# First layer in tiles of 512 columns, with all its work in one written order, on one Trainium2 core

## The chip, the core and the metric

The kernel is one program on one core of a Trainium2 chip. Five engines run their own instruction queues: PE (matrix multiply), DVE and ACT (vector and scalar work), POOL (a further elementwise engine), SP (which only issues DMAs here). An engine never leaves the order of its queue; an instruction that waits for a semaphore holds all behind it. The metric is the time of the program on the device in microseconds.

## What is computed

Attention of two kinds is added, then two feed-forward layers follow on 2304 tokens of 512 channels, all in float32:

```
# B, H, S, D = 4, 8, 576, 64; pooled: means over 4 tokens (144 per batch)
out_d = softmax(q_d k_d^T / 8) v_d            # pooled, per batch and head
local = softmax(q k^T / 8, |i - j| < 4) v      # 7 keys for each token
x     = repeat(out_d, 4) + local               # 2304 tokens x 512
h = x @ w_in; g = relu(h)**2; x2 = g @ w_out   # first layer, 2048 wide
y = ((x2 @ w_a) * (x2 @ w_b)) @ w_o2           # second layer, 1536 wide
```

The weights and the operands of the big products are split into a high and a low part, and a product is three matmuls: high by high, high by low, low by high (`PASSES`).

## The kernel before

**Tiles.** The first layer runs in nine tiles of 256 token columns. In each tile there are 16 steps f. Step f is `Hidden` (12 matmuls, line 598, into a PSUM bank), its `high` on ACT (relu, square and rounding, lines 606, 607, 609), its `low` on DVE (line 612), and, two steps later, `project` (12 matmuls, line 619, into two banks that collect over the 16 steps, two column blocks of 256 in each). The operands of a tile are the tiles `xx`; the result x2 goes to DRAM by way of `x2sb` (`x_d<-x2sb`), but for the last tile's, which stays on the chip (`xr`).

**Attention.** The first two tiles' local attention runs on PE (`Block`: scores, softmax, transposes, values); that of the other seven (`Local`) runs on DVE (products and sums, lines 379, 388, 419) and POOL (additions, lines 427 to 429) with its transposes on PE (line 436). Pooled attention (`Pooled`) runs once for each of four batches, in four pairs of heads: scores on PE (241, 256), minimum on DVE (268), exponentials with an accumulator read on ACT (278), division on ACT, POOL or DVE (293, 296), transposes (305) and values (319) on PE, copies on ACT or DVE. Its sums over 4 tokens are made by DMAs that add to what lies in the tile; POOL issues these (line 224). For batch 0 q and k go in two halves: `qkd` and two tiles `more`, each loaded by SP and added to by POOL's DMA, then joined by an addition (line 230).

**Weights.** Those of the first layer come packed; `wd` loads one of 32 pieces, `wc`, `wa`, `wh` and `wl` turn it into high and low parts on ACT, DVE and POOL.

**What sets the order.** A list of tokens (`ORDER`, 464 of them) gives the program order of the start and the first two tiles: block attention (`bq` to `bl`), batch 0 and part of batch 1 of the pooled attention (`pl` to `po`), the weights, and the steps `H`, `J` (`high`), `L` (`low`), `P` (`project`). From the third tile on a loop runs `H`, `J`, `L`, `P` for each step, and events by step number (`at_iteration`) place one piece of pooled or local attention beside each. Beside the last tile the second layer is prepared: its first weights are decoded (`wb`) and the first 1024 columns of x2 are loaded back (`x2s<-x_d`) and split (`xb`). The second layer runs in 512 columns (line 911), with sums and differences of blocks so that seven block products take the place of eight; ACT copies its banks out (line 1007, `r`), and among its first copies stand the splits of the next 1024 columns.

**PSUM.** Eight banks of 2 KB a partition: three for `Hidden`, two for the projection, three for attention. The first layer's banks are closed before the second layer opens its own eight.

## Time and profile before

| | us |
|---|---|
| median of 3 runs | 944.28 (943.98 to 947.16) |
| the profiled execution | 943.94 |
| its span, first to last instruction | 942.2 |
| first matmul of the first layer that is followed by more | 71.35 |
| first matmul of the second layer | 540.20 |

| busy in the span | us | share |
|---|---|---|
| PE | 891.4 | 95% |
| DVE | 620.4 | 66% |
| ACT | 480.7 | 51% |
| POOL | 355.3 | 38% |

The mean granted clock of PE over the span is 0.979 of full speed. A share over the whole span mixes three stretches: the attention of the start, the first layer, and the second layer; they are read apart below. Time that an engine other than PE is idle counts only where PE waits for it.

### The profile page before, as it was taken

The page shows a single profiled execution, that of the slowest core. Times are in us where ns is not written, and L with a number is a line of the kernel's source. Part 1 is how long each engine was busy: PE and PEld are TensorE (multiplying, and loading weights), DVE is VectorE, ACT ScalarE, POOL GpSimd, SP SyncE. Part 2 cuts the span into 40 slices and gives each one's busy share as a digit, 9 for nine tenths or more (in the row PEclk, how much of TensorE's full clock was granted, in tenths as well). Part 3 has the DMA queues.
Part 4 walks back from the last instruction along what each step waited for, and adds up shares of the span by engine and source line. Part 5 has one row for each costly group of instructions (what it writes and reads, how often), then busy time and mean ns, then how long its engine had stood idle before and what let it go on. Part 6 is the DMA issues. An engine that isn't in the chain of part 4 may idle for free.

```text
span 942.2 us, 16371 instructions
## 1 busy us (share of the span) xinstructions
PE 891.4 (95%) x6130; PEld 811.0 (86%) x6130; DVE 620.4 (66%) x892; ACT 480.7 (51%) x1232; POOL 355.3 (38%) x321
## 2 busy tenths in 40 slices
...
GB/s 312 168 164 248 263 115 90 155 140 65 81 63 204 99 82 63 74 71 69 96 90 103 120 50 190 267 275 201 226 211 184 254 168 351 387 407 357 227 101 79
DMA packets 69888, 161.86 MB, mean 172 GB/s; under 512 B 8472, under 2 KB 16920, under 8 KB 69808
## 3 DMA queue, kind: packets, MB, share of 16 engines
...
q8 instruction: 48, 0.79, 0.4%
q14 instruction: 32, 0.26, 0.1%
...
## 4 chain that ended last, share of the span: by engine, by line
PE 78%; DVE 6%; DMA 6%; ACT 4%; POOL 3%; issue 2%; ACTq 0%; SPq 0%; DVEq 0%; POOLq 0%
PE bank L911 39%; PE bank L619 18%; PE bank L598 18%; DMA more<-in_qk_p 2%; DMA raw<-in_w_in 1%; PE bank L241 1%; DMA wo<-wo_d 1%; DVE pv L419 1%; DMA ys<-y_d 1%; DVE p L379 1%; DVE g L612 1%; ACT a L278 1%; DMA qkd<-in_qk_p 1%; DVE raw L156 1%; POOL pv L428 1%
## 5 line engine op out<-in xcount | busy, mean ns | idle before, releaser
L598 PE MATMUL bank<-xx,w 128*128 128x256 f32 x1728 | 236.5, 287 | 10.2 <-DVE g L612 3.5
L619 PE MATMUL bank<-g,w 128*128 128x256 f32 x1728 | 233.8, 285 | 0.8 <-POOL w L167 0.4
L598 PEld LDWEIGHTS bank<-xx,w 128*128 128x128 f32 x1728 | 220.8, 194 | 14.1 <-DVE g L612 4.7
L911 PE MATMUL bank<-xb,wb 128*128 128x512 f32 x1008 | 230.4, 389 | 0.7 <-DVE r L961 0.5
L911 PEld LDWEIGHTS bank<-xb,wb 128*128 128x128 f32 x1008 | 188.6, 188 | 40.3 <-DVE r L961 1.5
L619 PEld LDWEIGHTS bank<-g,w 128*128 128x128 f32 x1728 | 216.3, 191 | 5.0 <-issue 2.9
L911 PE MATMUL bank<-op,wo 128*128 128x512 f32 (+1 forms) x648 | 132.1, 366 | 1.6 <-DVE op L772 1.6
L911 PEld LDWEIGHTS bank<-op,wo 128*128 128x128 f32 x648 | 111.9, 189 | 21.9 <-DVE op L772 2.3
L612 DVE TENSOR_TENSOR g<-bank,g 128x256 fp32r<-128x256 f32 x144 | 60.1, 420 | 99.5 <-ACT g L609 98.8
L427 POOL TENSOR_TENSOR pv<-pv 128x768 f32<-128x768 f32 x28 | 55.1, 1967 | 179.6 <-DVE pv L419 179.6
L606 ACT ACTIVATE bank<-bank 128x256 f32<-128x256 f32 x144 | 53.3, 370 | 120.3 <-PE bank L598 120.2
L772 POOL TENSOR_TENSOR wb<-raw,wb 128x256 fp32r<-128x256 f32 x96 | 83.0, 883 | 64.0 <-ACT wb L851 60.5
L1007 ACT ACTIVATE r<-bank 128x512 f32<-128x512 f32 x72 | 43.0, 597 | 93.8 <-PE bank L911 84.8
L772 DVE TENSOR_TENSOR op<-ys,op 128x512 fp32r<-128x512 f32 x84 | 54.0, 707 | 31.3 <-ACT op L775 31.3
L156 DVE SCALAR_TENSOR_TENSOR raw<-raw,signs 128x512 uint32<-128x512 uint32 x68 | 57.6, 852 | 25.1 <-ACT signs L129 23.4
L961 DVE TENSOR_TENSOR r<-bank,r 128x512 f32<-128x512 f32 x48 | 32.8, 686 | 43.9 <-PE bank L911 31.0
L419 DVE TENSOR_TENSOR pv<-vt,sc 128x1792 f32<-128x1792 f32 x28 | 58.6, 2100 | 3.0 <-POOL x L429 3.0
L775 ACT ACTIVATE op<-ys 128x512 fp32r<-128x512 f32 x84 | 47.1, 624 | 25.6 <-PE bank L911 15.0
L379 DVE TENSOR_TENSOR p<-qt,kt 128x1792 f32<-128x1792 f32 x28 | 60.2, 2149 | 0.0
L609 ACT ACTIVATE g<-bank 128x256 fp32r<-128x256 f32 x144 | 55.4, 385 | 4.6
L388 DVE TENSOR_REDUCE sc<-p 128x28 f32<-128x1792 f32 x28 | 56.1, 2004 | 0.0
L772 POOL TENSOR_TENSOR wos<-raw,wos 128x256 fp32r<-128x256 f32 x48 | 43.6, 924 | 31.5 <-ACT wos L851 29.4
...
## 6 DMA issues: line engine op xcount, KB each, us to landing
...
y_d<-r SPq DMA_DIRECT2D x72, 256.0 KB, 2.0
wo_d<-wos SPq DMA_DIRECT2D x48, 256.0 KB, 2.4
...
wo<-wo_d SPq DMA_DIRECT2D x24, 256.0 KB, 7.5
...
```

The source lines that it names most:

```text
L156: nc.vector.scalar_tensor_tensor(out=self.v, in0=self.v, scalar=13, in1=self.signs, op0=ALU.logical_shift_right, op1=ALU.bitwise_or,)
L379: nc.vector.tensor_tensor(out=self.p, in0=q.unsqueeze(2).to_broadcast([P, FACTOR, WIN, D]), in1=window(k), op=ALU.mult,)
L388: nc.vector.tensor_reduce(out=self.s[:, :, h], in_=self.p, axis=AX.X, op=ALU.add)
L419: nc.vector.tensor_tensor(out=p, in0=window(heads.pop(("v", n))), in1=self.s[:, :, h].unsqueeze(3).to_broadcast([P, FACTOR, WIN, D]), op=A ...
L427: add(out=p[:, :, 0:3], in0=p[:, :, 0:3], in1=p[:, :, 4:7], op=ALU.add)
L598: nc.tensor.matmul(out=h, lhsT=wi[f].w[:, a, ct * P:(ct + 1) * P], rhs=x_rhs(i, ct, b), start=(n == 0), stop=(n == 3 * NCT - 1),)
L606: nc.scalar.activation(out=h, in_=h, func=AF.Relu)
L609: nc.scalar.activation(out=self.g[:, 0], in_=h, func=AF.Copy)
L612: nc.vector.tensor_tensor(out=self.g[:, 1], in0=self.h, in1=self.g[:, 0].bitcast(F32), op=ALU.subtract)
L619: nc.tensor.matmul(out=x2[et // 2][:, et % 2 * T1:(et % 2 + 1) * T1], lhsT=wo[f].w[:, a, et * P:(et + 1) * P], rhs=g[:, b], start=(f == 0 ...
L772: engine.tensor_tensor(out=out, in0=in0, in1=in1, op=ALU.subtract)
L911: nc.tensor.matmul(out=out, lhsT=blk[:, a, cols:cols + P], rhs=rhs[b], start=(start and n == 0), stop=(stop and n == 2), skip_group_check= ...
```

## The change

**Tiles.** The first layer now runs in five tiles: 512, 256, 512, 512 and 512 columns (`TILES`). Two or one of the 256-token pieces of attention make the operands of one tile. Each of the 16 steps is again 12 + 12 matmuls. `Hidden` alternates between two PSUM banks, the projection collects in four (one for each 128 channels), attention has two. `project` does the passes with the high part of g first, then those with the low part; the first `Hidden` of a tile does the same with its operands.

**Blocks.** Three pieces of local attention run on PE (`BLOCKS`); `Local` runs for pieces 3 to 8.

**Order.** One list of 1197 tokens sets the order of everything up to the second layer: also all pooled and local attention, the evictions of x2 (`E`), its stores (`D`), the opening of the second layer's pools (`Q`), the parts of its preparation (`F`), and the last 256 columns' halves (`rh`, `rl`). The loop and its events are gone. In the last tile, pieces 7 and 8 end together: piece 7 is stored, piece 8 stays on the chip.

**Loads.** All loads of the start are issued by SP (before, ACT issued some of them). Pooled q and k of batch 0 are eight plain loads and six additions; the other batches keep the adding DMAs.

The core of the diff:

```diff
-PE_TILES = 2
+BLOCKS = 3
+TILES = ((0, 2), (2, 1), (3, 2), (5, 2), (7, 2))
+LAST = len(TILES) - 1
...
-        def add_more(self, n, j):
-            src = qk_p[self.b, j][:, n * NCT * SG:(n + 1) * NCT * SG]
-            self.add_to(self.more[n], src, j % 2)
...
+        def get(self, n, j, queue):
+            if j == 0:
+                out = (self.qd, self.kd)[n]
+            else:
+                out = self.more[n, j] = wp.tile([P, NCT * SG], F32, tag="w", name="more")
+            queue.dma_start(out=out, in_=qk_p[self.b, j][:, n * NCT * SG:(n + 1) * NCT * SG])
 
-        def join(self, n, engine):
+        def join(self, n, j, engine):
             d = (self.qd, self.kd)[n]
-            engine.tensor_tensor(out=d, in0=d, in1=self.more[n], op=ALU.add)
+            engine.tensor_tensor(out=d, in0=d, in1=self.more.pop((n, j)), op=ALU.add)
...
     class Hidden:
-        def __init__(self, i, f):
-            self.h = h = bank("h")[:, :T1]
...
+        def __init__(self, t, f):
+            width = TILES[t][1] * T1
+            self.h = h = bank((t * F1 + f) % 2)[:, :width]
+            todo = [(ct, a, b) for ct in CTS[t] for a, b in PASSES]
+            if f == 0:
+                todo.sort(key=lambda z: z[2])
+            for n, (ct, a, b) in enumerate(todo):
+                nc.tensor.matmul(
+                    out=h, lhsT=wi[f].w[:, a, ct * P:(ct + 1) * P], rhs=xT[t, ct][:, b],
...
+    def project(t, f):
         if f == 0:
-            x2[i] = [bank(kind) for kind in kinds]
...
+            width = TILES[t][1] * T1
+            x2[t] = [bank(2 + et)[:, :width] for et in range(NCT)]
+        g = hid.pop((t, f)).g
+        todo = [(et, a, 0) for et in range(NCT) for a in range(2)] + [(et, 0, 1) for et in range(NCT)]
+        for et, a, b in todo:
...
+    def store(t, e2):
+        i, count = TILES[t]
+        if t == LAST:
+            count -= 1
+            src, ets = x2sb[t, 0], slice(0, NCT)
```

**Three places in the order.** First, POOL at the start. `qkd` and `more` are pooled q and k, `vd` pooled v, `blk` the blocks' exponentials; a DMA row is an issue, and the DMAs on POOL add to what lies there. Before:

```order
L224 DMA more<-in_qk_p 128x576
L224 DMA vd<-in_v_p 72x1024
L224 DMA qkd<-in_qk_p 128x1152
L224 DMA more<-in_qk_p 128x576
L527 TENSOR_TENSOR blk<-blk,den 128x560
L230 TENSOR_TENSOR qkd<-qkd,more 128x576
L527 TENSOR_TENSOR blk<-blk,den 128x560
```

Now:

```order
L1377 DMA vd<-in_v_p 72x1024
L1390 TENSOR_TENSOR qkd<-qkd,more 128x576
L1685 TENSOR_TENSOR blk<-blk,den 128x560
L1390 TENSOR_TENSOR qkd<-qkd,more 128x576 x3
L1685 TENSOR_TENSOR blk<-blk,den 128x560 x2
L1350 TENSOR_TENSOR w<-raw,w 128x512
L1377 DMA vd<-in_v_p 72x1024
```

The adding DMAs for q and k are gone from here, and three more joins have come; the loads they join are SP's rows:

```order
L1379 DMA vd<-in_v_p 72x1024
L1386 DMA qkd<-in_qk_p 128x576 x2
L1386 DMA more<-in_qk_p 128x576 x3
L1624 DMA qb<-in_q_t 128x1024
L1628 DMA kb<-in_k_t 128x524 x2
L1630 DMA band<-in_mask 128x140
L1386 DMA more<-in_qk_p 128x576 x3
L1330 DMA raw<-in_w_in 128x2047
```

`raw` is a piece of weights; before, SP's first rows held one part of each (`more`, `vd`, `qkd`, `raw`, `more`), and the rest came by POOL.

Second, PE in the middle of the first layer. L1766 and L1801 are `Hidden` and `project` of the new code (before L598 and L619), L1399 pooled scores, L1453 and L1591 transposes of pooled and local attention (before L305 and L436), L1467 pooled values. Before, from the third tile on, in this manner:

```order
L598 MATMUL bank<-xx,w 128x256 x12
L305 MATMUL bank<-ident,a 72x72 x4
L619 MATMUL bank<-g,w 128x256 x12
L598 MATMUL bank<-xx,w 128x256 x12
L305 MATMUL bank<-ident,a 72x72 x4
L436 MATMUL xps<-ident,x 128x128 x4
L619 MATMUL bank<-g,w 128x256 x12
L598 MATMUL bank<-xx,w 128x256 x12
L619 MATMUL bank<-g,w 128x256 x12
L598 MATMUL bank<-xx,w 128x256 x12
L319 MATMUL bank<-aT,vd 64x144 x4
L256 MATMUL bank<-qkd 72x144 x4
```

Now, between the last projection of the second tile and the first hidden matmuls of the third:

```order
L1591 MATMUL bank<-ident,x 128x128 x4
L1399 MATMUL bank<-qkd 72x144 x4
L1453 MATMUL bank<-ident,a 72x72 x8
L1467 MATMUL bank<-aT,vd 64x144 x4
L1453 MATMUL bank<-ident,a 72x72 x8
L1467 MATMUL bank<-aT,vd 64x144 x4
L1591 MATMUL bank<-ident,x 128x128 x4
L1467 MATMUL bank<-aT,vd 64x144 x4
L1453 MATMUL bank<-ident,a 72x72 x8
L1467 MATMUL bank<-aT,vd 64x144 x4
L1591 MATMUL bank<-ident,x 128x128 x4
L1766 MATMUL bank<-xx,w 128x512 x24
```

The attention pieces, which stood one or two at a time between groups of twelve, stand in a row here; ahead of this piece are the tile's last 36 projections with eight pooled score matmuls and eight transposes between them. The ends of the first and the third tile have like rows; at the end of the fourth only three groups of four transposes stand between the last projections.

Third, the border of the layers. On SP, `x_d<-x2sb` stores x2, `x2s<-x_d` loads it back, `raw` are weights. Before:

```order
L644 DMA x_d<-x2sb 128x2x256 x2
L349 DMA vt<-in_v_l 128x640 x2
L147 DMA raw<-in_w_a 128x2047 x2
L789 DMA x2s<-x_d 128x512 x8
L644 DMA x_d<-x2sb 128x2x256 x2
L147 DMA raw<-in_w_b 128x2047 x2
L789 DMA x2s<-x_d 128x512 x8
L147 DMA raw<-in_w_a 128x2047 x2
L147 DMA raw<-in_w_b 128x2047 x2
L955 DMA y_d<-r 128x512 x5
```

Now:

```order
L1330 DMA raw<-in_w_b 128x2047 x2
L1830 DMA x_d<-x2sb 128x2x512
L1877 DMA x2s<-x_d 128x512 x8
L1830 DMA x_d<-x2sb 128x2x512
L1330 DMA raw<-in_w_a 128x2047 x2
L1830 DMA x_d<-x2sb 512x1x256
L1877 DMA x2s<-x_d 128x512 x8
L1330 DMA raw<-in_w_a 128x2047 x2
L1330 DMA raw<-in_w_b 128x2047 x2
L2081 DMA y_d<-r 128x512 x5
```

The last store (512x1x256: piece 7, all channels) stands ahead of the second eight loads, and weights and a store that stood elsewhere lie around it. On ACT, `r` is the copy of a second-layer bank, `xb` the split of x2. Before:

```order
L609 ACTIVATE g<-bank 128x256
L851 ACTIVATE wb<-raw 128x256
L775 ACTIVATE xr_6532<-bank 128x512
L775 ACTIVATE xr_6535<-bank 128x512
L1007 ACTIVATE r<-bank 128x512
L775 ACTIVATE xb<-x2s 128x512 x2
L1007 ACTIVATE r<-bank 128x512
L775 ACTIVATE xb<-x2s 128x512 x2
L1007 ACTIVATE r<-bank 128x512
L775 ACTIVATE xb<-x2s 128x512 x2
```

Now:

```order
L1296 ACTIVATE x2sb<-bank 128x256
L1939 ACTIVATE wb<-raw 128x256
L1838 ACTIVATE xr_4762<-bank 128x256 x2
L1296 ACTIVATE x2sb<-bank 128x256 x2
L1838 ACTIVATE xr_4770<-bank 128x256 x2
L2133 ACTIVATE r<-bank 128x512
L1863 ACTIVATE xb<-x2s 128x512 x2
L2133 ACTIVATE r<-bank 128x512
L1863 ACTIVATE xb<-x2s 128x512 x2
L2133 ACTIVATE r<-bank 128x512
```

Evictions of the last tile (`x2sb`) have come in ahead of the second layer's first copy; the copies and splits behind are in the order of before.

## Rows read from the trace of the kernel before

**Rows 1.** The page's chain of work that ended last, by line

```profile
PE bank L911 39%; PE bank L619 18%; PE bank L598 18%; DMA more<-in_qk_p 2%; DMA raw<-in_w_in 1%; PE bank L241 1%; DMA wo<-wo_d 1%; DVE pv L419 1%; DMA ys<-y_d 1%; DVE p L379 1%; DVE g L612 1%; ACT a L278 1%; DMA qkd<-in_qk_p 1%; DVE raw L156 1%; POOL pv L428 1%
```

**Rows 2.** Busy time by stage: stretch, its length, busy us (instructions), granted clock, DMA

```profile
71.35:150.00 78.65, 70.58 (x528) 65.25 (x528) 60.22 (x87) 55.24 (x146) 32.37 (x28) 0.92 0.69 204
150.00:540.20 390.20, 386.77 (x3273) 380.16 (x3273) 270.04 (x355) 198.99 (x568) 156.86 (x116) 1.00 0.35 96
```

**Rows 3.** Timeline of PE at full clock: start, duration, line, tiles, count

```profile
499.88 1.60 PE L598 MATMUL bank<-xx,w 128*128 128x256 f32 x12
501.32 1.60 PE L619 MATMUL bank<-g,w 128*128 128x256 f32 x12
...
613.79 15.57 PE L911 MATMUL bank<-xb,wb 128*128 128x512 f32 x68
629.21 5.92 PE L911 MATMUL bank<-xr,wb 128*128 128x256 f32 x48
```

**Rows 4.** The page's costliest groups, first layer: busy, mean, idle before

```profile
L598 PE MATMUL bank<-xx,w 128*128 128x256 f32 x1728 | 236.5, 287 | 10.2 <-DVE g L612 3.5
L619 PE MATMUL bank<-g,w 128*128 128x256 f32 x1728 | 233.8, 285 | 0.8 <-POOL w L167 0.4
```

**Rows 5.** The chain that ended last, in order of time, at the start

```profile
18.80 13.47 DMA more<-in_qk_p
...
67.29 5.97 DMA qkd<-in_qk_p
```

**Rows 6.** Timeline of POOL at the start

```profile
32.40 1.40 POOL L230 TENSOR_TENSOR qkd<-qkd,more 128x576 f32<-128x576 f32 x1 [9.43 <-DMA more<-in_qk_p]
33.76 1.31 POOL L527 TENSOR_TENSOR blk<-blk,den 128x560 f32<-128x560 f32 x1
```

**Rows 7.** Timeline of PE: pooled scores, and the first layer's first matmuls

```profile
37.82 1.98 PE L241 MATMUL bank<-qkd 64*72 64x144 f32 x12
...
71.35 1.44 PE L598 MATMUL bank<-xx,w 128*128 128x256 f32 x5 [1.95 <-DVE xx L580]
...
77.09 5.28 PE L598 MATMUL bank<-xx,w 128*128 128x256 f32 x29 [0.37 <-POOL xx L580]
```

**Rows 8.** The page's DMA rate in 40 slices of the span

```profile
GB/s 312 168 164 248 263 115 90 155 140 65 81 63 204 99 82 63 74 71 69 96 90 103 120 50 190 267 275 201 226 211 184 254 168 351 387 407 357 227 101 79
```

**Rows 9.** Timeline of ACT: four normalising operations of one pooled head pair

```profile
131.39 1.32 ACT L293 ACTIVATE a<-a,den 72x144 f32<-72x144 f32 x4
```

**Rows 10.** Groups by form: line, engine, tiles, count, busy us, mean ns, idle

```profile
L278 ACT ACTIVATE a<-bank,mx 72x144 f32<-72x144 f32 x64 | 23.5, 372 | 22.4 <-DVE mx L268 22.3
...
L268 DVE TENSOR_REDUCE mx<-bank 72x2 f32<-72x288 f32 x32 | 14.2, 445 | 10.6 <-PE bank L241 10.5
...
L278 ACT ACTIVATION_READ_ACCUMULATOR a<-bank,mx 72x1 f32 x64 | 12.5, 195 | 0.0
...
L129 ACT ACTIVATE aT<-bank 72x288 f32<-72x288 f32 x28 | 11.1, 399 | 6.9 <-PE bank L305 2.8 <-POOL w L167 2.5 <-PE bank L319 1.5
...
L296 POOL TENSOR_TENSOR a<-a,den 72x576 f32<-72x576 f32 x3 | 4.4, 1474 | 1.9 <-DVE den L286 1.9
```

**Rows 11.** Busy time and granted clock in two stretches of the start

```profile
44.00:80.00 36.00, 24.32 (x168) 18.94 (x169) 17.06 (x36) 23.01 (x60) 20.22 (x20) 0.53 0.72 193
...
92.00:100.00 8.00, 6.35 (x38) 5.92 (x39) 5.76 (x9) 6.45 (x15) 2.82 (x3) 0.79 0.57 131
```

**Rows 12.** Timeline of PE behind an idle time of the first layer

```profile
93.55 4.90 PE L598 MATMUL bank<-xx,w 128*128 128x256 f32 x24 [2.47 <-DVE g L612]
98.28 1.60 PE L619 MATMUL bank<-g,w 128*128 128x256 f32 x12
```

**Rows 13.** The page's DMA issues: tile, queue, count, KB each, us to landing

```profile
x_d<-x2sb SPq DMA_DIRECT2D x16, 256.0 KB, 2.2
x2s<-x_d SPq DMA_DIRECT2D x16, 256.0 KB, 2.7
```

**Rows 14.** Timeline of ACT: first copy of a second-layer bank

```profile
541.79 0.60 ACT L1007 ACTIVATE r<-bank 128x512 f32<-128x512 f32 x1 [0.79 <-PE bank L911]
```

More of the change, by code (lines that the diff above doesn't have):

```diff
@@ L68 @@
[L68 removed]
+sg
+bq.0.S
+pl.0
+pa.0.1.0
+pg.0.1.0.S
+bs.0.0.0.3
+pg.0.0.0.S
+pg.0.1.2.S
+bs.0.1.1.7
+bm.0.0.0
+bs.0.0.1.5
+pg.0.1.1.S
+pg.0.0.2.S
+bm.0.0.1
+pa.0.1.1
+bq.1.S
+bs.0.1.0.6
+pj.0.1.1.G
+bx.0.0
+pg.0.0.1.S
+bs.1.1.1.2
+bm.0.1.1
+bs.1.0.1.5
+bm.0.1.0
+pj.0.1.2.V
+be.0.0
+bx.0.1
+bd.0.0
+pg.0.0.3.S
+bs.1.0.0.4
+be.0.1
+bd.0.1
+pg.0.1.3.S
+bm.1.0.1
+bn.0.0.G
+bm.1.0.0
+pj.0.0.1.V
+pj.0.1.3.G
+bx.1.0
+pj.0.0.2.G
+bs.1.1.0.5
@@ new lines @@
+pw.1.2.6
+pc.1.3.0.A
+ba.2.0.G
+po.1.2.A
+pc.1.3.1.V
+pw.1.3.2
+po.1.3.A
+bh.2.1.V
+bh.2.0.V
+ba.2.1.G
+bh.2.2.A
+bl.2.1.V
+bl.2.2.G
+bl.2.0.V
+bh.2.3.A
+bl.2.3.V
+H.1.0
+lk.15
+pl.2
+lu.13
+ls.4.1
+H.1.1
+lu.12
+lm.3.3
+J.1.0
+L.1.0
+E.0.2.A
+pa.2.1.0
+P.1.0
+pa.2.0.0
+J.1.1
+H.1.2
+J.1.2
+ls.3.3
+L.1.1
+P.1.1
+lm.4.3
+L.1.2
+H.1.3
+D.0.1
+lx.3
+H.1.4
+le.3
+P.1.2
+pa.2.0.1
+J.1.3
+lz.3
+lb.4
+lk.18
+L.1.3
+H.1.5
+P.1.3
+J.1.4
+lv.3.0
+L.1.4
+H.1.6
+P.1.4
+lu.14
+J.1.5
+ls.4.3
+L.1.5
+H.1.7
+P.1.5
@@ new lines @@
+lv.3.1
+J.1.6
+pa.2.1.1
+pa.2.0.2
+L.1.6
+H.1.8
+lk.16
+J.1.7
+lw.3.0
+P.1.6
+lm.4.2
+pa.2.0.3
+lu.17
+pa.2.1.2
+L.1.7
+H.1.9
+J.1.8
+P.1.7
+pq.2.A
+ps.2.0.1.6
+lk.23
+ls.4.2
+lw.3.1
+lm.4.0
+L.1.8
+J.1.9
+H.1.10
+P.1.8
+lv.3.2
+L.1.9
+P.1.9
+D.0.0
+H.1.11
+lu.15
+px.2.0.1
+J.1.10
+ls.4.0
+L.1.10
+ps.2.0.0.7
+J.1.11
+lx.4
+H.1.12
+lw.3.2
+P.1.10
+lv.3.3
+le.4
+L.1.11
+H.1.13
+P.1.11
+lz.4
+J.1.12
+pa.2.1.3
+L.1.12
+H.1.14
+lw.3.3
+lu.16
+J.1.13
+P.1.12
+lv.4.1
+L.1.13
+lk.22
+px.2.0.0
+H.1.15
+J.1.14
@@ new lines @@
+J.2.1
+L.2.1
+P.2.1
+H.2.3
+J.2.2
+L.2.2
+P.2.2
+H.2.4
+lm.5.2
+pa.3.0.0
+J.2.3
+L.2.3
+P.2.3
+H.2.5
+pa.3.0.1
+J.2.4
+lk.20
+L.2.4
+P.2.4
+H.2.6
+ls.5.3
+lm.5.0
+pa.3.0.2
+J.2.5
+pa.3.1.0
+L.2.5
+H.2.7
+ls.5.2
+pa.3.0.3
+pq.3.A
+ps.3.1.0.6
+ps.3.1.1.7
+P.2.5
+J.2.6
+lk.25
+ls.5.0
+lk.21
+lm.5.1
+lk.27
+L.2.6
+H.2.8
+px.3.1.1
+ls.5.1
+lx.5
+P.2.6
+pe.3.1.1
+pa.3.1.1
+ps.3.0.1.7
+lm.6.1
+J.2.7
+ls.6.1
+J.2.8
+le.5
+lk.24
+L.2.7
+H.2.9
+lb.6
+lz.5
+P.2.7
+L.2.8
+H.2.10
+P.2.8
+J.2.9
+lm.6.3
+lv.5.1
@@ new lines @@
+P.3.4
+H.3.6
+J.3.5
+ls.7.1
+lm.8.3
+J.3.6
+lm.7.3
+D.2.0
+L.3.5
+P.3.5
+H.3.7
+ls.7.3
+lk.34
+ls.8.3
+lx.7
+L.3.6
+P.3.6
+lk.33
+le.7
+H.3.8
+lz.7
+J.3.7
+J.3.8
+lv.7.1
+lm.8.1
+L.3.7
+P.3.7
+H.3.9
+ls.8.1
+lk.32
+lu.28
+lm.8.2
+L.3.8
+P.3.8
+lb.8
+D.2.1
+lw.7.1
+H.3.10
+lv.7.2
+J.3.9
+ls.8.2
+L.3.9
+P.3.9
+lm.8.0
+lw.7.2
+H.3.11
+J.3.10
+lv.7.0
+L.3.10
+H.3.12
+P.3.10
+lw.7.0
+lu.34
+J.3.11
+ls.8.0
+lx.8
+lt.7.0.7
+lu.31
+le.8
+lv.7.3
+lw.7.3
+L.3.11
+P.3.11
+lu.35
+J.3.12
+H.3.13
+lt.7.1.6
+lz.8
@@ new lines @@
+L.4.2
+H.4.3
+J.4.3
+P.4.2
+L.4.3
+H.4.4
+Q
+J.4.4
+L.4.4
+P.4.3
+H.4.5
+P.4.4
+F.4.0
+J.4.5
+L.4.5
+H.4.6
+D.3.1
+F.1.0
+P.4.5
+J.4.6
+L.4.6
+F.2.0
+H.4.7
+P.4.6
+H.4.8
+F.6.0
+J.4.7
+L.4.7
+P.4.7
+F.6.1
+H.4.9
+J.4.8
+L.4.8
+P.4.8
+H.4.10
+D.3.0
+J.4.9
+L.4.9
+P.4.9
+H.4.11
+F.0.0
+J.4.10
+L.4.10
+P.4.10
+F.5.0
+F.5.1
+H.4.12
+F.7.0
+F.3.0
+F.6.2
+J.4.11
+F.3.1
+L.4.11
+P.4.11
+F.6.3
+H.4.13
+F.7.1
+F.5.2
+F.5.3
+J.4.12
+L.4.12
+P.4.12
+F.7.2
+H.4.14
+F.7.3
+F.7.4
+F.7.5
+F.6.4
+F.3.2
+F.5.4
```

1428 lines of the change are left out of this document (1085 added, 343 removed).

## The prediction

> **What bounds the kernel now.** I read first the chain of work that ended last, by line [rows 1]: three PE lines, the second layer's (L911) and the first layer's two (L598, L619), hold 75% of the span. Then the busy time by stage [rows 2]: from the first hidden matmuls at 71.35 us to 150 us PE is busy 70.58 of 78.65 us at 0.92 of its clock, from 150 to 540.2 us 386.77 of 390.20 at 1.00. So the first layer is PE's work, back to back, and can get shorter only if its matmuls do, or if it starts earlier. The second layer's 402 us (540.2 to 942.2) are the same code in both kernels, except where they begin.
>
> What a matmul costs is read from where groups of them start at full clock [rows 3]: twelve 256-column matmuls take 501.32 - 499.88 = 1.44 us, 120 ns each; 68 of 512 columns take 629.21 - 613.79 = 15.42 us, 226.8 ns each. At 2.4 GHz the columns alone would be 106.7 and 213.3 ns, so each matmul has about 13.3 ns that do not grow with its width.
>
> The first layer then splits so: 71.35 to 540.2 is 468.9 us; its 3456 matmuls [rows 4] by 120 ns are 414.7; the other 54.2 us are 11.0 of idle before the two lines (10.2 and 0.8 in the same rows), and 43 of attention on PE and of matmuls at the lower clock.
>
> **Part 1, columns.** 4 of the 5 new tiles have 512 columns, one 256. Matmuls: 4 x 16 x 24 = 1536 wide and 384 narrow. 1536 x 0.2268 + 384 x 0.120 = 394.4 us against 414.7: **-20.3 us**. This is on the bounding engine and nothing hides it. Against that stands a rule. The Trainium skill, TensorE: Matmul & The Clock Gate, section "Wait — 56ns, not 53.3ns?", gives a warm matmul a fixed cost of about 2.5 ns; by it the 1536 matmuls fewer would bring only 3.8 us. The trace disagrees with the 2.5 (13.3 at both widths, [rows 3]); what it would mean is rival D.
>
> **Part 2, the start.** Before, the pooled scores wait for a chain of accumulating loads, the last of which takes 13.47 us and ends at 32.3 [rows 5]; then POOL joins at 32.40 [rows 6] and the scores run at 37.82 [rows 7]. The change loads eight plain parts, and joins them on DVE and POOL. The bytes queued up to the last part are two blocks' q, k and band, one v and eight parts of 0.29 MB, about 4.8 MB; at the 312 GB/s of the first slice [rows 8] they are in at 16 to 17 us. Four joins on POOL at 1.40 us, with a block step of 1.31 between them [rows 6], end near 22 if the first can run while the last parts come in; the scaling brings the scores to about 23.5: 14.3 us earlier. The work from the scores to the first hidden matmul (37.82 to 71.35) I keep at its length, 33.5 us, so that the first layer starts at about 57: **-14.3 us**. Bounds: -20, because POOL's later wait for a pooled load (5.97 us from 67.29 [rows 5]), which parts the first hidden matmuls until 77.09 [rows 7], is also gone; and -5 if weight decode, whose loads now queue on SP alone behind the 4.8 MB, is what comes last. I take the middle one since the ops between are the same.
>
> **Part 3, what PE does beside the matmuls.** This is where the change loses. Before, a 256-column tile's attention sits piecewise between groups of twelve matmuls, and the next tile's operands are ready long before. Now a 512-column tile needs twice the operands at once, and at the ends of tiles 0 to 2 the order puts the last attention steps in one row, with no matmul of the layer between them; at the end of tile 3 a few stand between the last projections. At each such place PE waits for a chain on ACT, and I price it by ACT's ops: four normalising ops 1.32 us [rows 9], one exponential with its accumulator read 0.56 us pitch (0.372 and 0.195, [rows 10]), a copy of 288 columns 0.40 [rows 10], which I take for all copies of 256 to 288.
> - End of tile 0: the third block's tail, one pooled head pair: minimum 0.45, two exponentials 1.13, POOL's normalising 1.47 [rows 10]; transposes, copy, values, output, adding and halves are nine steps that I estimate at the copy's 0.40, with 1 us for the hand-overs: 7.7 us.
> - End of tile 1: on ACT 16 normalising ops (5.3), 12 exponentials (6.8), and 16 copies, for eight operand halves, three evictions, three transposed copies and two outputs (6.2 to 6.4): 18.4 us, less 4.8 of projections (36 narrow matmuls) and scores that PE still has and 0.9 of slack: 12.7.
> - End of tile 2: the same kinds, 17.0 less 3.9 less 0.9: 12.2.
> - End of tile 3: only the last local transposes' additions and copies, six steps at the copy's 0.40: 2.5.
>
> That is 35 us of gaps; the attention that still runs between matmuls outside of them is about 18 us (about half of the 43 above without its clock part). Stalls outside the gaps I leave at what before shows, 11 idle. The clock: from 44 to 80 us the granted clock was 0.53 after PE had done little, and from 92 to 100 us 0.79 [rows 11], after an idle time of 2.47 us; there 24 narrow matmuls took 98.28 - 93.55 = 4.73 us instead of 2.88 [rows 12], 1.9 us lost. Three gaps and the first hidden tile: 4 x 2 = 8. Together 35 + 18 + 11 + 8 = 72 against 54.2: **+18 us**. Bounds on the 72: 55 if the gaps shrink to half, because the softmax ops of the next tile are done while PE still has projections; 92 if no step of the chains overlaps PE's work.
>
> On the clock the Trainium skill's section "What's actually happening" in TensorE: Matmul & The Clock Gate says that the gate falls back to 1.2 GHz after idleness, a rule that speaks against a change with long gaps; [rows 11] agree in both stretches, and the 8 us rest on [rows 12].
>
> **Part 4, the junction.** Before, the second-last tile's x2 was stored a tile ahead of the second layer. Now blocks 7 and 8 end together: block 7's store comes after the last projection, four evictions and the first remainders. A store takes 2.2 us, a load back 2.7 [rows 13]; behind the store SP's queue holds the loads of the second span. ACT issues the operand copies of these loads between the copies of the second layer's first banks, which before began 1.6 us after its first matmul [rows 14]. About 2.5 + 2.2 + 2.7 us after the last projection the first operands are there, and PE meets the uncopied bank about 4 us earlier than it is free: +4. Preparation steps now stand in the same ACT and DVE rows as the last f's: +3. Sum **+7**, bounds 0 (the copies do not wait) and +12 (the whole latency and its clock).
>
> **Sum.** 943.9 (the profiled execution) - 20.3 - 14.3 + 18 + 7 = 934.3; the median lies 0.3 above that execution: **935**.
>
> **The rivals.** About 0.5%, 939.6 to 949.0, is what a measurement here can tell from no change.
> - B, the attention is further ahead than I think: the gaps of 35 us come to half, 17 us less: 918. For it: ACT was busy 198.99 of 390.20 us and DVE 270.04 [rows 2]. Against: the order puts the steps late, and an engine does not leave its order.
> - C, slower: the gaps take the whole ACT chains (8, 18, 17 and 6 at tile 3, 49 in place of 35), and as they pass to PE and back, PE's own small steps in them, about 1.5 us at each place, come on top: 20 us over my sum, 955. It decides when the first layer's remainder passes 54.2 + 20.3 + 14.3 - 7 = 82 us. For it: PE cannot begin a wide tile with half of its operands, and the projection's last groups are few. Against: hi-first ordering lets the first hidden matmuls start before the low halves are there.
> - E, the early start does not do what it says: the first hidden matmul stays near 71 because decode of the weights or the block attention decides: 949.
> - D, the wide matmuls of this layer, whose data come from other tiles than the second layer's, keep the narrow ones' rate per column (120 / 256 ns, 240 each): part 1 gains nothing, 955. For it: no wide matmul of this layer is in the trace. Against: L911's at 226.8 [rows 3]. By the 2.5 ns of the Trainium skill's section named in part 1 that part would gain 3.8 us, and the time be 951.
>
> **How the numbers follow.** Chances: mine 0.46 (930 to 942 on its own sizes), B 0.26, C 0.13, E 0.12, D 0.03. Faster by over 0.5%: B whole and some seven tenths of mine, with little of E: 0.61. Same: three tenths of mine, half of E: 0.20. Slower: C, D and the rest of E, with mine at its upper bound: 0.19. The range must leave out no more than 2 in 10: from 914 (B, with a start of -18) to 953 (E whole, and the milder part of C).
>
> **What would show it.** Columns: first-layer groups of twelve 512-column matmuls 2.72 us apart. Start: pooled scores near 23 us, first hidden matmul that counts at 55 to 60; at 66 or more part 2 is wrong. Gaps: at four places PE idle with ACT as the releaser, 35 us in all, with a granted clock under 1 behind them; under 20 us is B, over 50 is C. Junction: the first second-layer bank copies on ACT separated by several us, PE idle on a bank. What would make it wrong in kind: a tile in which DVE and not PE is the bound, or weights, which SP alone now loads, that come too late for tile 0.

## The result: 1.0% slower, and the profile after

The changed kernel takes 954.69 us (median of 4 executions, 953.67 to 956.46); the kernel before, run beside it, 945.39. The ratio is 1.0099, with a 95% interval of 1.0072 to 1.0127: **slower by 1.0%**. The prediction said 935, with a range up to 953 that does not hold this. The profiled execution of after took 955.61 us, its span is 953.8 (before 943.94 and 942.2), so the two traces differ by 11.6 us, and every one of them can be placed. Among all runs one execution is set aside as slow, one of e12's twelve below (1472.64 us at a granted clock of 0.573); the median of e12 counts it, its ratio does not.

The page's chain by line (the line that answers to [rows 1]):

```profile
PE bank L2037 37%; PE bank L1766 17%; PE bank L1801 15%; POOL pv L1583 2%; DVE pv L1573 1%; PE bank L1399 1%; PE bank L1467 1%; DMA vd<-in_v_p 1%; POOL pv L1584 1%; PE bank L1453 1%; DVE sc L1541 1%; PE bank L1709 1%; DMA y_d<-r 1%; POOL x L1585 1%; DMA ys<-y_d 1%
```

A store, `y_d<-r`, holds 1% of the chain; among the entries of [rows 1] there is no store. Keep this one in mind: it is what the prediction missed.

Busy time by stage, the answer to [rows 2]: stretch, its length, then busy us (instructions) of PE, weight loads, DVE, ACT and POOL, granted clock, DMA share, GB/s:

```profile
61.65:150.00 88.35, 88.35 (x454) 71.27 (x453) 63.70 (x104) 50.94 (x112) 30.24 (x30) 1.00 0.60 182
150.00:532.86 382.86, 369.05 (x1878) 301.61 (x1877) 264.56 (x318) 167.33 (x409) 148.43 (x113) 0.95 0.32 85
```

The first stretch has become gapless at the full clock. The second has become worse: 13.8 us idle instead of 3.4, at 0.95 of the clock instead of 1.00.

The 11.6 us, laid out from PE's timelines of both kernels:

| where | predicted | measured (after - before) |
|---|---|---|
| part 1, columns of the first layer | -20.3 | -17.1 |
| part 2, first hidden matmul | -14.3 | -9.7 (61.65 for 71.35) |
| part 3, what PE does beside these matmuls | +18 | +19.4 |
| part 4, junction of the layers | +7 | +6.2 |
| second layer, behind its first product, to the end | 0 | **+12.8** |
| sum | -9.6 | +11.6 |

Part 1 is counted from the spacing of the matmul groups, and part 3 is what the first layer's length leaves beside it. Part 4 is read at the second layer's first matmuls of 256 columns, below under the junction; what is behind them is the last line.

**The start.** PE's timeline (start, duration, line, tiles, count) with a pooled score piece, and the first tile:

```profile
37.17 1.23 PE L1399 MATMUL bank<-qkd 64*72 64x144 f32 x4
...
61.65 6.12 PE L1766 MATMUL bank<-xx,w 128*128 128x512 f32 x24
67.61 2.88 PE L1801 MATMUL bank<-g,w 128*128 128x512 f32 x12
```

The first hidden matmul is at 61.65, 9.7 us ahead of [rows 7]. Its 24 matmuls take 67.61 - 61.65 = 5.96 us, near the full-clock 5.44 (24 x 226.8 ns).

**The gaps.** PE around the end of the second tile, and the granted clock of two gaps, of the second and the third tile (same columns as above):

```profile
219.79 0.71 PE L1399 MATMUL bank<-qkd 64*72 64x144 f32 x4
...
225.24 0.71 PE L1467 MATMUL bank<-aT,vd 72*64 72x144 f32 x8
...
228.21 1.23 PE L1467 MATMUL bank<-aT,vd 72*64 72x144 f32 x8
...
237.68 7.76 PE L1766 MATMUL bank<-xx,w 128*128 128x512 f32 x22 [0.95 <-ACT xx L1607]
245.28 1.99 PE L1801 MATMUL bank<-g,w 128*128 128x512 f32 x8
```

```profile
215.00:245.00 30.00, 26.68 (x153) 20.02 (x152) 20.14 (x41) 16.52 (x60) 18.45 (x14) 0.72 0.38 82
330.00:360.00 30.00, 28.50 (x159) 21.55 (x158) 19.13 (x34) 18.98 (x58) 13.55 (x10) 0.83 0.18 53
```

From 219.79 to 237.68 PE does attention pieces and two hidden matmuls: 18 us, and PE is busy for 14.6 of them, but eight pooled value matmuls take 0.71 us at 225.24 and 1.23 at 228.21. Behind it 22 matmuls take 245.28 - 237.68 = 7.60 us, 2.6 more than 22 x 226.8 ns.

**The junction.** PE, then ACT, then SP (issue, how long, how many); in brackets the idle time before and what ended it:

```profile
532.86 7.09 PE L2037 MATMUL bank<-xb,wb 128*128 128x512 f32 x30 [1.32 <-ACT x2sb L1296]
543.81 11.20 PE L2037 MATMUL bank<-xb,wb 128*128 128x512 f32 x42 [3.86 <-ACT r L2133]
...
559.38 5.92 PE L2037 MATMUL bank<-xr,wb 128*128 128x256 f32 x48
```

```profile
542.64 0.63 ACT L1863 ACTIVATE xb<-x2s 128x512 fp32r<-128x512 f32 x1 [4.87 <-DMA x2s<-x_d]
543.18 0.58 ACT L2133 ACTIVATE r<-bank 128x512 f32<-128x512 f32 x1
```

```profile
532.83 0.60 SPq L1830 DMA_DIRECT2D x_d<-x2sb  x1
533.53 5.97 SPq L1877 DMA_DIRECT2D x2s<-x_d  x8
```

The bank copy at 543.18 stands in ACT's order behind the operand copy at 542.64, and that waited 4.87 us for a load that queued up behind the store at 532.83. PE pays 3.86 us for it, and the 42 matmuls behind take 11.2 us, 1.7 more than 42 x 226.8 ns. In before the 72 matmuls run through:

```profile
540.20 16.51 PE L911 MATMUL bank<-xb,wb 128*128 128x512 f32 x72
...
560.53 5.92 PE L911 MATMUL bank<-xr,wb 128*128 128x256 f32 x48
```

From the first product to the first 256-column matmuls of the layer that is 559.38 - 532.86 = 26.52 us for 20.33, the +6.2 of the table.

**The place that was not foreseen.** PE near the end of the second layer's first part, in after:

```profile
765.79 32.83 PE L2037 MATMUL bank<-xb,wb 128*128 128x512 f32 x144
808.05 8.03 PE L2037 MATMUL bank<-xb,wb 128*128 128x512 f32 x24 [9.43 <-ACT r L2133]
815.92 1.14 PE L2037 MATMUL bank<-op,wo 128*128 128x512 f32 x4
```

and in before, one run of 168 matmuls:

```profile
766.54 38.27 PE L911 MATMUL bank<-xb,wb 128*128 128x512 f32 x168
804.65 1.17 PE L911 MATMUL bank<-op,wo 128*128 128x512 f32 x4
```

ACT and SP of after at that place, and a piece of its chain in order of time:

```profile
807.40 1.08 ACT L2133 ACTIVATE r<-bank 128x512 f32<-128x512 f32 x2 [13.59 <-DMA y_d<-r]
```

```profile
788.55 8.32 SPq L2190 DMA_DIRECT2D ys<-y_d  x8
797.78 0.32 SPq L2081 DMA_DIRECT2D y_d<-r  x1
```

```profile
797.78 9.46 DMA y_d<-r
```

Read it from PE backwards. PE waits 9.43 us for a bank that ACT is to copy into an `r` buffer. ACT waits 13.59 us, not for the bank but for a store `y_d<-r`: the buffer still holds an older result that has to leave first. SP issues that store only at 797.78, behind eight 512 KB loads, and it lands 9.46 us later. The 24 matmuls behind the wait take 7.87 us instead of 5.44.

SP and ACT of before at the same place:

```profile
788.66 8.17 SPq L1064 DMA_DIRECT2D ys<-y_d  x8
797.77 0.32 SPq L955 DMA_DIRECT2D y_d<-r  x1
```

```profile
798.10 0.60 ACT L1007 ACTIVATE r<-bank 128x512 f32<-128x512 f32 x1 [3.53 <-PE bank L911]
```

There the store is issued behind the same eight loads at 797.77, as late as in after. But ACT copies its bank at 798.10, as soon as PE has filled it: its buffer does not wait for that store.

Why the buffer is that one stands in lines of the diff that lie far from the first layer and are not among those shown ahead of the prediction:

```diff
-                        r[n] = xp.tile([P, 2, HALF], F32, tag="x", name="r")
+    def quad(shape, name):
+        turns[0] += 1
+        return xp.tile(shape, F32, tag=f"x{turns[0] % 4}", name=name)
...
+                        r[n] = quad([P, 2, HALF], "r")
```

Before, `r1`, `r2` and `r3` came from a pool of four under one tag, and took, as I read the program, whichever buffer had been released first. Now four buffers, each with its own tag, are taken in strict turn. Each pass of the second layer's first part takes three, so by the turn each `r3` falls on the buffer of the `r2` of the pass before; for the last pass that store is the late one. (The traces leave buffer numbers out: which buffer it is comes from the code; that the turn makes the wait is what e1 and e4 test.)

### The profile page after: what moved, and what is told of

It is laid out like the page before. It is cut to its first block, busy times and chain, and to the rows that moved or that the text cites. A ratio compares the mean times of both kernels' runs of the same rounds, so it can differ in the third digit from the quotient of the medians.

```text
span 953.8 us, 13396 instructions
## 1 busy us (share of the span) xinstructions
PE 901.4 (95%) x4728; PEld 745.7 (78%) x4728; DVE 614.6 (64%) x872; ACT 437.4 (46%) x1040; POOL 338.9 (36%) x315
## 4 chain that ended last, share of the span: by engine, by line
PE 75%; DVE 9%; DMA 5%; POOL 4%; issue 3%; ACT 2%; SPq 0%; DVEq 0%; ACTq 0%; POOLq 0%
PE bank L2037 37%; PE bank L1766 17%; PE bank L1801 15%; POOL pv L1583 2%; DVE pv L1573 1%; PE bank L1399 1%; PE bank L1467 1%; DMA vd<-in_v_p 1%; POOL pv L1584 1%; PE bank L1453 1%; DVE sc L1541 1%; PE bank L1709 1%; DMA y_d<-r 1%; POOL x L1585 1%; DMA ys<-y_d 1%
## 5 line engine op out<-in xcount | busy, mean ns | idle before, releaser
L2037 PE MATMUL bank<-xb,wb 128*128 128x512 f32 x1008 | 235.1, 394 | 15.9 <-ACT r L2133 13.3
L1766 PE MATMUL bank<-xx,w 128*128 128x512 f32 (+1 forms) x960 | 222.6, 383 | 6.6 <-DVE g L1781 4.3
L1801 PE MATMUL bank<-g,w 128*128 128x512 f32 (+1 forms) x960 | 212.0, 370 | 0.0
L1766 PEld LDWEIGHTS bank<-xx,w 128*128 128x128 f32 x960 | 173.3, 196 | 44.4 <-DVE g L1781 6.6
L1801 PEld LDWEIGHTS bank<-g,w 128*128 128x128 f32 x960 | 167.4, 189 | 31.4 <-issue 1.3
L1773 ACT ACTIVATE bank<-bank 128x512 f32<-128x512 f32 (+1 forms) x80 | 43.2, 540 | 179.1 <-PE bank L1766 175.7
L1781 DVE TENSOR_TENSOR g<-bank,g 128x512 fp32r<-128x512 f32 (+1 forms) x80 | 50.5, 632 | 95.0 <-ACT g L1776 87.6
L1583 POOL TENSOR_TENSOR pv<-pv 128x768 f32<-128x768 f32 x24 | 47.4, 1976 | 124.1 <-DVE pv L1573 119.5
L1533 DVE TENSOR_TENSOR p<-qt,kt 128x1792 f32<-128x1792 f32 x24 | 49.8, 2080 | 4.1 <-POOL x L1585 4.0
L1776 ACT ACTIVATE g<-bank 128x512 fp32r<-128x512 f32 (+1 forms) x80 | 44.4, 555 | 9.9 <-PE bank L1801 7.9
L1541 DVE TENSOR_REDUCE sc<-p 128x28 f32<-128x1792 f32 x24 | 48.0, 2007 | 0.1
```

The lines of the kernel that those rows point to most:

```text
L1533: nc.vector.tensor_tensor(out=p, in0=q.unsqueeze(2).to_broadcast([P, FACTOR, WIN, D]), in1=window(k), op=ALU.mult,)
L1541: nc.vector.tensor_reduce(out=self.s[:, :, h], in_=self.p.pop(h), axis=AX.X, op=ALU.add)
L1583: add(out=p[:, :, 0:3], in0=p[:, :, 0:3], in1=p[:, :, 4:7], op=ALU.add)
L1766: nc.tensor.matmul(out=h, lhsT=wi[f].w[:, a, ct * P:(ct + 1) * P], rhs=xT[t, ct][:, b], start=(n == 0), stop=(n == 3 * NCT - 1),)
L1776: nc.scalar.activation(out=self.g[0], in_=h, func=AF.Copy)
L1781: nc.vector.tensor_tensor(out=self.g[1], in0=h, in1=self.g[0].bitcast(F32), op=ALU.subtract)
```

## The experiments

Theory: the four parts do about what was predicted, and the strict turn of the `r` buffers takes the gain away. Rivals: the wait at 798 us comes from the changed preparation of the second layer (other loads and evictions in front of it), or the junction is what costs. Then the sizes of parts 1 to 4 were tested each by itself. An experiment named as "on e3" or "on e5" has all edits of that one.

### e1: the r buffers in order of release

After, with `r3` on a buffer of its own and `r1`, `r2` rotating in the other three, which I take to be the order in which before's pool gave them out:

```diff
-                        r[n] = quad([P, 2, HALF], "r")
+                        r[n] = kept(n, [P, 2, HALF])
```

> The changed kernel with one thing undone: the second layer's r buffers are taken in the order in which they come free, as before, and no longer in strict rotation over four (r3 gets r3's old buffer; r1 and r2 share the other three). Theory (rotation): the last column span's r3 waits for the store of the previous span's r2, which is issued behind eight loads of 512 KB and lands at 807 us; with the other buffer the 9.4 us of PE idle at 798 us and the low clock behind it go, 12 us less: about 942 to 943, and PE runs from 560 us to the last stage without a gap. Rival (full queue): the DMA queue is what is late there, the wait only names it; PE then stops a little later for the loads themselves, and the time stays at 950 or more.

Measured: 943.99 us, ratio to before 0.9995 [0.9982, 1.0008]. PE of e1 at the place of the wait:

```profile
765.07 38.27 PE L2042 MATMUL bank<-xb,wb 128*128 128x512 f32 x168
803.17 1.17 PE L2042 MATMUL bank<-op,wo 128*128 128x512 f32 x4
```

The wait is gone, 168 matmuls run through, and `op` begins at 803.17 instead of 815.92. This one line is worth 10.7 us of the median. Without it the change is neither faster nor slower. Other buffers of the second layer that the change hands out in turn as well (six tags, for `c` and `t6` among others) keep their turn in e1, so they are not the cause.

### e4: the kernel before with the strict turn

The mirror image. Nothing of the change but the turn, in the kernel before, for all tiles of that pool, the first layer's too:

```diff
-    xp = ctx.enter_context(tc.tile_pool(name="xp", bufs=4))
+    xq = ctx.enter_context(tc.tile_pool(name="xp", bufs=1))
...
+            Rotated.n += 1
+            return xq.tile(shape, dtype, tag=f"x{Rotated.n % 4}", name=name)
+
+    xp = Rotated()
```

> The kernel before with that one part of the change alone: all tiles of its pool of four are taken in strict rotation, the first layer's too, where they come free in that order anyway. Theory (rotation): a gap of PE at about 799 us as in the changed kernel, 10 to 12 us more: 955 to 957. Rival (full queue, or the list order of the first layer brings it): 944 to 946, as before.

Measured: 955.39 us, 1.0122 [1.0099, 1.0146]. Its PE, its SP, and its chain at the same place:

```profile
809.55 7.57 PE L920 MATMUL bank<-xb,wb 128*128 128x512 f32 x24 [8.48 <-ACT r L1016]
```

```profile
791.03 7.34 SPq L1073 DMA_DIRECT2D ys<-y_d  x8
```

```profile
799.32 9.48 DMA y_d<-r
```

The same wait, the same store behind the same eight loads, in a kernel whose start, first layer and junction are before's (its second layer begins at 541.63 instead of 540.20): `op` begins at 816.95 instead of 804.65. Cost and gain mirror each other (+10.9 and -10.7 of the medians; e2 and e3 below, run side by side, differ in the `r` buffers alone and lie 11.2 apart). With e1 this shows the cause from both sides, and the rival that the changed preparation makes the wait falls.

### e2 and e3: the splits of the second operands later

The wait of 3.86 us in the junction: ACT's operand copies moved from the first product's row of the plan to the fourth. e2 does it in after, e3 in e1.

```diff
-    put(1, [fn for pair in zip(units[1, 0][1:], units[1, 1][1:]) for fn in pair], 2)
+    put(4, [fn for pair in zip(units[1, 0][1:], units[1, 1][1:]) for fn in pair], 2)
```

> The changed kernel with the splits of the second 1024 columns (xb) put four in place of one slot behind the start of the second layer, so that ACT's first copies of banks don't stand behind splits that wait for the late store and its loads. Theory (ACT's order): PE's idle of 3.9 us at 540 us and most of the 1.1 us behind go, with the low clock after it: 4 to 6 us less, about 949. Rival (the loads are late whatever the order): the operands come too late for the second span's first products at about 560 us, and PE waits there instead; no gain, 953 to 955.

> Both edits of the two runs before this. Theory: the two gaps lie 250 us apart and add: 12 + 5, about 937, 0.8% faster than the kernel before. Rival: one hides part of the other (a start of the second layer that is 5 us earlier meets the same DMA queue), 942 or more.

Measured: e2 954.0 us, 1.0105 [1.0075, 1.0135]; e3 942.8, 0.9984 [0.9972, 0.9995]. PE of e3:

```profile
534.54 16.61 PE L2042 MATMUL bank<-xb,wb 128*128 128x512 f32 x72 [1.32 <-ACT x2sb L1296]
...
569.46 15.38 PE L2042 MATMUL bank<-xb,wb 128*128 128x512 f32 x60 [2.21 <-ACT r L2138]
```

The 72 matmuls run through, so the wait in the junction does come from ACT's order. But a new wait of 2.21 us stands at 569.46, where ACT does the copies it now has late. From the first product to the second matmul group of `op` e3 needs 272.75 us (534.54 to 807.29), e1 273.76 (532.15 to 805.91), before 267.19 (540.20 to 807.39): of some 6 us that the junction costs, the edit gives 1.0 back. Neither the expected 949 (e2) nor 937 (e3) was reached; the rival of e2, no gain, is what came.

### e5 and e12: dense matmuls in the gaps

On e3: in the gaps behind the second and the third tile, six times each, ahead of an attention piece, the matmuls of `Hidden`'s form into the piece's own bank, which the piece then overwrites (four of 256 columns, or two of 512). e12 is the same kernel on another chip.

```diff
-pn.2.1.A pt.2.1.0.6
+pn.2.1.A z.1.4 pt.2.1.0.6
```

> On the kernel with both edits (r buffers by release, splits later): dense matmuls of the layer's own kind, whose result is overwritten, are put ahead of six attention pieces at the end of tile 1 (four of 256 columns each) and six at the end of tile 2 (two of 512 each); nothing else waits for them. They cost 2.9 and 2.7 us of PE at full clock. Theory (PE's clock): the attention pieces in these two gaps run at half rate because the clock falls, and with the clock kept at 2.4 GHz the two gaps and the first hidden matmuls behind them shrink by 4 to 8 us more than the fillers cost: 936 to 939. Rival (ACT's and DVE's chain is the bound, as I had predicted): PE only waits longer between its pieces, no change to +5: 943 to 948.

> The kernel with dense matmuls in the gaps at the ends of tiles 1 and 2 again, on the chip of the run before this, for a comparison of the two and for the spread between executions, which was 937.7 to 947.1. Theory (the dense matmuls are worth about 3 us): median near 939 to 941, below the kernel before. Rival (the low median of its first measurement was chance): 942 to 944.

Measured: 939.62 us, 0.9962 [0.994, 0.9985], and again 939.63, 0.9951 [0.9932, 0.9971]. The two stretches in e5, and PE on both sides of the first gap:

```profile
215.00:245.00 30.00, 26.72 (x192) 21.11 (x192) 22.84 (x43) 18.19 (x65) 19.23 (x14) 1.00 0.37 82
330.00:360.00 30.00, 28.32 (x175) 21.26 (x174) 19.31 (x34) 18.73 (x58) 11.90 (x9) 1.00 0.15 49
```

```profile
220.94 0.71 PE L306 MATMUL bank<-qkd 64*72 64x144 f32 x4
...
238.11 5.59 PE L673 MATMUL bank<-xx,w 128*128 128x512 f32 x22 [1.34 <-ACT xx L514]
```

The clock stays at 1.00 and the pieces at 0.71 us, and still the gap is 238.11 - 220.94 = 17.2 us long, against 17.9 in e3 (221.03 to 238.91). In both PE is idle for 3.3 us of it: the dense matmuls took up about as much of PE as the faster pieces gave back, 13.9 us busy for 14.6. So this run does not tell whether PE's pieces or the chain over ACT and DVE set the length of a gap. What the clock costs stands behind it: 22 matmuls in 5.4 us (238.11 to 243.54) instead of 8.0 in e3 and 7.6 in after. Behind the other gap less came back: from its first piece to the end of the 24 hidden matmuls 19.2 us (335.44 to 354.66) for 20.0 in e3. This kernel beats after by 1.6% and before by 0.4 to 0.5%: the lowest median of the study.

### e6: whose chain? The divisions on DVE

On e3: six of the normalising steps in the two gaps from ACT to DVE (`pn.2.1` to `pn.2.3`, `pn.3.1` to `pn.3.3`). My sum in part 3 had counted ACT alone.

```diff
-pn.2.1.A
+pn.2.1.V
```

> On the kernel with both edits: six of the divisions of pooled attention at the ends of tiles 1 and 2 (each four ACT operations of 1.32 us together) are one DVE operation of about 0.75 us each. Theory of the prediction (ACT's sum bounds the gaps): ACT loses 4 us in each gap, the gaps shrink by 2 to 3 us each, 938 to 940. Rival (the chain goes from PE to ACT to DVE and back and PE's own pieces at half rate are most of it): under 2 us in all, 941 to 943; DVE, which has Local work in the same place, may make it worse.

Measured: 949.97 us, 1.0062 [1.0041, 1.0083], 7 us slower than e3. The longest of PE's waits in the first of the two gaps:

```profile
225.90 0.69 PE L342 MATMUL bank<-ident,a 72*72 72x72 f32 x8 [2.02 <-DVE a L333]
```

ACT has 3 x 1.32 = 4 us [rows 9] less to do in each gap; the first one lasts 19.5 us (219.94 to 239.45) instead of 17.9, and PE waits for DVE in it. So the sum of ACT's ops does not set the length of a gap: with 4 us less of them it got longer. In after's gap (219.79 to 237.68) ACT is busy for 10.3 us, DVE for 12.9 and PE for 14.6 of 17.9; which of them a shorter gap would need first is not shown.

### e7: the wide matmuls as halves

On e3: each 512-column matmul of the first layer as two of 256, everything else the same. This measures part 1 by itself.

```diff
+                for c in range(0, width, T1):
-                    out=h, ... rhs=xT[t, ct][:, b],
+                    out=h[:, c:c + T1], ... rhs=xT[t, ct][:, b, c:c + T1],
```

> On the kernel with both edits: every 512-column matmul of the first layer is issued as two of 256 columns, all else as it is, so 1536 matmuls more. Theory (13.3 ns for each matmul, whatever its width): +20 us, 962 to 964. Rival (a small fixed cost of 2.5 ns, or a cost that goes by columns): +4 or less, 943 to 947.

Measured: 955.02 us, 1.0113 [1.0089, 1.0136], 12.2 us above e3. Groups of PE in the last tile, of e7 and then of after:

```profile
470.75 3.04 PE L1804 MATMUL bank<-g,w 128*128 128x256 f32 x24
473.63 3.04 PE L1767 MATMUL bank<-xx,w 128*128 128x256 f32 x24
```

```profile
463.38 2.88 PE L1766 MATMUL bank<-xx,w 128*128 128x512 f32 x12
466.10 2.88 PE L1801 MATMUL bank<-g,w 128*128 128x512 f32 x12
```

There the groups are 2.88 and 2.72 us apart, and 0.16 us by 12 matmuls is the forecast 13.3 ns each. In the other three wide tiles after's pair takes 5.51 us instead of 5.44, and e7's at 80 to 97 us and at 380 to 420 5.73 to 5.74: about 9 ns. By groups that makes 16 x 0.32 + 48 x 0.22 = 15.7 us; the medians show 12.2. By the 2.5 ns of the Trainium skill (TensorE: Matmul & The Clock Gate, section "Wait — 56ns, not 53.3ns?") the 1536 matmuls more would make 3.8 us, an estimate: the measurement decides against it here. Rival D (nothing gained) falls by the 12.2 too.

### e8: is the start bound by PE?

On e3: two matmuls of the 128 x 128 identity ahead of 17 of the attention pieces before the first hidden matmul, to see whether PE has room there and whether the pieces get faster. (The trace counts the two as four.)

```diff
-px.0.2.0 ps.0.0.1.7
+px.0.2.0 zi.2 ps.0.0.1.7
```

> On the kernel with both edits: two dense 128-column matmuls, overwritten later, ahead of every second one of 34 attention pieces on PE before the first hidden matmul (34 in all, about 0.2 us each at full clock, 7 us in all). Theory (PE's half rate bounds the start from 37 us on, where PE is busy without a gap and each piece takes twice as long as at full clock): if these matmuls keep the clock up, the start shrinks by 3 to 10 us; if they do not, it grows by 7 to 14. Rival (loads, weight decode or ACT bound the start): the first hidden matmul stays near 62 us, within 3 us, in either case.

Measured: 962.17 us, 1.0191 [1.0166, 1.0216]. PE of e8:

```profile
47.42 1.22 PE L204 MATMUL bank<-ident 128*128 128x128 f32 x4
...
79.70 5.84 PE L673 MATMUL bank<-xx,w 128*128 128x512 f32 x24
```

17 additions of 1.0 to 1.2 us move the first hidden matmul by 18 us, from 61.57 (e3) to 79.70: not one of them fits beside other work (7 us were expected for all). From 37 us on, the start is PE's own pieces, not loads, weights or DVE. The additions did not make the pieces faster.

### e9, e10, e11: three that did not pay

e9, on e5: two dense matmuls ahead of four pieces at the end of the first tile too (`po.1.0.A` becomes `po.1.0.A z.0.2`, and so on).

> The kernel with dense matmuls in the gaps at the ends of tiles 1 and 2, and now also ahead of four attention pieces at the end of tile 0 (two of 512 columns each, 1.8 us). Theory (what the dense matmuls give back is the low clock behind a gap): behind this gap 20 narrow matmuls took about 4.6 us in place of 2.4, so 2 us less: about 938. Rival (the chain at the end of tile 0 runs through PE, and the fillers delay it): 0 to 2 us more, 939 to 942.

Measured: 944.6 us, 1.0002 [0.9978, 1.0025], single executions between 939.9 and 949.5. In the profiled one the 20 narrow matmuls behind the gap, at 167.26, are as slow as in after (4.76 us, 4.77 there). The additions that kept the clock in the other two gaps did nothing in this one. The profiled execution is the fastest of the ten (939.9), so no trace shows what made the others slower. I have no reason for it, nor for the spread.

e10, on e9: the third block's attention, which stands in front of the first hidden matmul, moved into the first tile (`bs.2.0.0` and its successors behind `P.0.0`).

> As the run before, and the third block's scores, masks, exponentials, normalising and first transposes (about 6 us of PE pieces at half rate, 64 small score matmuls and 8 transposes) come between the first hidden and projection groups of tile 0 in place of ahead of the first hidden matmul. Theory (PE at half rate bounds the start): the first hidden matmul comes 5 to 6 us earlier, near 56 us; the pieces cost about 3 us at full rate in the layer: 2 to 3 us less, 935 to 937. Rival (weight decode or the operands bound the first hidden matmul once these pieces are gone, or ACT's exponentials hold up the first hidden steps): the start gains under 2 us or tile 0 loses what it gains, 938 or more.

Measured: 949.4 us, 1.0058 [1.0034, 1.0082]. PE of e10:

```profile
101.74 0.47 PE L708 MATMUL bank<-g,w 128*128 128x512 f32 x1 [1.69 <-DVE w L188]
```

The first hidden matmul comes 2 us earlier than in e9 (58.61 for 60.49), but the tile then runs into its weights, which DVE and POOL decode beside the moved steps. What the third block costs in front, it hides for the weights. This is read from the slowest of six executions (955.23, the median is 949.4).

e11, on e5: one step of local attention on DVE (`lv.5.2`) behind a step of the layer instead of in front of it, since PE waits 2.93 us for it at 318 us in after (`<-DVE g L1781`).

```diff
-lv.5.2 L.2.12
+L.2.12 lv.5.2
```

> The kernel with the r buffers by release, the later splits and the dense matmuls at the ends of tiles 1 and 2, and one exchange in the order of DVE in tile 2: step 12's low half comes ahead of a Local value product (lv.5.2), which waits 1.95 us for POOL and behind which the low half, and with it PE's bank, waited. Theory (an op that waits holds what is behind it on its engine): PE's idle of 2.95 us at 316 us and the twelve matmuls at half rate behind it (4.4 in place of 2.8 us) go, 4 us less than the kernel without the exchange, 935 to 937. Rival (DVE is the bound of tile 2 and the value product's delay comes back at the end of the tile through POOL's sums and the last transposes): under 1 us.

Measured: 944.69 us, 0.9996 [0.9973, 1.002], single executions from 938.6 to 951.5. PE of e11:

```profile
331.52 1.21 PE L708 MATMUL bank<-g,w 128*128 128x512 f32 x4 [1.03 <-DVE g L688]
...
353.90 7.07 PE L673 MATMUL bank<-xx,w 128*128 128x512 f32 x24
```

The wait at 318 us is gone. Its work comes up again before the gap (1.03 us at 331.52), and in this execution the gap ran at the slower pace in spite of the dense matmuls, 24 matmuls behind it taking 6.9 us.

## Why the prediction was wrong, step by step

**The step that failed** is one sentence of the first part: "The second layer's 402 us (540.2 to 942.2) are the same code in both kernels, except where they begin." They are not; their buffers are handed out differently, and that is +12.8 us (9.43 of waiting, some 2.4 of slower matmuls behind it, little else). The page row of before hides it:

```profile
y_d<-r SPq DMA_DIRECT2D x72, 256.0 KB, 2.0
```

2.0 us from issue to landing as a median, while the one store that matters is issued behind eight loads of 512 KB. SP's timeline of before shows that (788.66 and 797.77 above); who holds the buffer had to be read from the diff. With that line undone the kernel takes 943.99 us (e1): inside the range, but 9 us over the forecast, so the other steps are not all right either.

**Part 1, right in its rule, too large:** -17.1 for -20.3. The last wide tile has its groups 2.72 us apart, as forecast. In the other three a hidden and a projecting group together take 5.51 us instead of 5.44, so 48 x 5.51 + 16 x 5.44 + 384 x 0.120 = 397.6 us, not 394.4. Why these three are 0.07 us slower a pair is open.

**Part 2, right in sign, too large:** -9.7 for -14.3. The pooled scores began at 27.67 us, not 23.5. POOL in after:

```profile
19.12 1.40 POOL L1390 TENSOR_TENSOR qkd<-qkd,more 128x576 f32<-128x576 f32 x1 [2.98 <-DMA more<-in_qk_p]
21.22 2.88 POOL L1390 TENSOR_TENSOR qkd<-qkd,more 128x576 f32<-128x576 f32 x2 [0.69 <-DVE qkd L1390]
```

The last part was there at 19.1, not at 16 to 17 (queue and rate were too hopeful), and the last join ended at 24.1. The 33.5 us that I kept from the scores to the first hidden matmul came to 34.0. But they were kept for no good reason: before, PE was idle for 8.4 of them; now it is busy in all of them from 37 us on, with pieces at half pace (1.23 us for 0.71). e8 shows that it is PE that bounds them now.

**Part 3, right in size, wrong in kind:** +19.4 for +18 (the remainder is 471.2 - 397.6 = 73.6 where I had 72). The gaps, from the last projection to the first hidden matmul that runs on, are about 7, 18, 13 and 3 us where I had 7.7, 12.7, 12.2 and 2.5; 8 us for the clock was about 2.2, 2.6, 1.2 and 0.5, together 6.5. Two things were off and cancelled: the gap of the second tile was 5 us longer, and less attention was left outside of gaps. But the sign that I named, PE idle with ACT as the releaser for 35 us in all, did not come. PE's idle time in the stretches of the four gaps is 1.45, 3.32, 1.50 and 1.78 us, 8 in all (148 to 168, 215 to 245, 330 to 360, 430 to 450), with ACT, DVE, POOL and a DMA as releasers. For the rest of the gaps PE works at its own attention pieces, part of them at half pace. The sum had nothing for these pieces in the gaps, and it took 1 us for hand-overs and 0.9 of slack that no row gave; that ACT's ops came out near the length is luck as far as the runs tell (e6). By my own sign (under 20 us of idle) this would have been rival B, but its time did not come: the gaps are 41 us, not half of 35. Rival C's time, 955, was hit by the measurement, but by another mechanism: its gaps of 49 us did not come, and the remainder stayed at 73.6, under the 82 at which C decides.

**Part 4, right in size:** +6.2 for +7. The store and load chain came as described, only longer: 3.48 us for the store, 4.97 for a load, where [rows 13] have 2.2 and 2.7. The wait was 3.86 us for the +4; the +3 for preparation steps had no row, and what stands beside the wait is mostly the slower pace behind it, 1.7 us. The mechanism is only in part ACT's order: moved away, it comes back one span later (e3).

**Rival E** (the start gains nothing) is refuted, and "slower" had 0.19 by rivals of which none was the cause.
